# Two units' decay factors loaded once and spread by TensorE, with a new instruction sequence

## Chip, cores and metric

The kernel runs on one core of a Trainium2 chip. The metric is the device time of one execution in microseconds (us), the median of several runs. Engines are called as in the profile: PE is TensorE (PEld its weight loads), DVE is VectorE, ACT is ScalarE, POOL is GpSimd, SP is SyncE, which here only issues DMAs. "SP's queue", "ACT's queue" and "POOL's queue" are the DMA queues that these engines issue to.

## What is computed

A chunked state-space layer (batch 4, 8 heads, 768 steps, head dimension 32, state 16) is followed by a SiLU feed-forward block (256 to 2048 to 256) on its 3072 output rows:

```python
cum = np.cumsum(log(clip(a, 1e-6, 1)), axis=-1)          # within a chunk
L = np.exp(cum[..., :, None] - cum[..., None, :]) * causal
y = (einsum(C, B) * L) @ x + (C @ state) * exp(cum)
state = exp(sum(la)) * state + sum(B x x * exp(cum[-1] - cum))
...
h = y_rows @ w_in
out = (h * (1 / (1 + exp(-h)))) @ w_out
```

`a`, `B`, `C` and `x` are float32. The two weight matrices are float64, and the kernel reads them as pairs of 32-bit words.

## The kernel before

**Units.** The work is cut into 12 units of 256 steps, three for each batch element; a unit has four chunks of 64 steps. The feed-forward part takes units two at a time: a pair has 512 rows. The first pair (units 0 and 1) is multiplied in plain float32, the other five in a split form with three passes (h, l, d).

**The order is written out.** The string `SCHEDULE` is a list of steps such as `E,0,0` or `Ln,1,1,1,0`. A loop calls the function of each step, and each engine runs its instructions in the order in which they were issued. Steps of different engines have no order but by their data and their buffers. `SLOTS` says which buffer of a pool each new tile takes; a buffer taken again makes its new writer wait for the last reader.

**The steps of a unit u**, with the names used below:
- `Ln,u,i,k` loads half k of B (i = 0) or C (i = 1) with time on the partitions; `Lt,0,1,g` loads a quarter of unit 0's C in another layout; `Lx,u,k` loads half of x. A step's last number is its queue: 0 SP, 1 ACT, 2 POOL.
- `E,u,k` (DVE, a scan of 512 elements) builds the decay matrix of half k from a. `P` or `P01` (DVE, a scan of 260) builds the running products of a within each chunk.
- `T,u,i` transposes on DVE, `tp,u` on PE (units 0 to 2). `tq,u` and `ce,u,e` (ACT) copy the results out, `ce` masked for even or odd heads. `C,u` multiplies C by the running products, `B,u,k` B by the last column of the decay matrix (POOL).
- `g0,u` and `D,u` or `gd,u` (PE) form C times B and B times x; `M,u,w` (DVE) multiplies by the decay; `S,u,t` (DVE) carries the state from chunk to chunk; `SM,u,e` (ACT) masks it; `Y,u` (PE) forms the unit's output. `X0` or `y` copies that out (ACT).

**The weights.** `lw,n` (n = 0 to 15) loads a block of 512 KB. `u,n` and `v,n` (ACT), `w,n,0` to `w,n,2` (DVE) and `W,n` (POOL) turn it into float32. `H,n` (ACT), `Wl,n` (POOL), `Wd,n` (ACT) and `We,n` (a DMA on POOL's queue) make the split parts.

**The feed-forward part.** `s,u,j` is the first product of unit u (0 or 1) with weight block j, in 8 PE instructions; `si,u,j` its SiLU. `n,k` is k products of 2 PE instructions each of the second matrix for the first pair. `a,G,i`, `d,G,i` and `f,k` are the same for the other pairs. PE thus has a fixed list of work, and what can vary is how early it starts and how often it waits.

**a, for units 0 and 1.** The decay factors of the later units come through DRAM copies that the kernel writes itself (`ir`, `AA`, `AD`, then `La` and `Lp`). For units 0 and 1 they are made in two ways. `ip,u` (line 346) loads a unit's a to all 128 partitions, 16 copies of each head, 128 KB for each unit; `P01,u,0` (line 442) clamps it and `P01,u,1` (line 446) scans it. `ia` (line 342) loads the same values once more, 16 KB, as 32 rows; `A` (line 415) clamps them, `AT` transposes them on PE, `AU` copies them out, `as,u,k` (line 466, one on DVE, three on ACT) repeats each value 64 times, and `ab,u,k` (line 471) turns that in four PE transposes into a PSUM tile that holds on each row the factors of its chunk. `E` scans that tile.

`z,k,m` (lines 408 and 410) are products on constant data that feed nothing: k of 512 columns, m of 64.

Of the kernel before, what the change touches and what calls it, by code (L numbers as in the profile page):

```python
# [13 lines left out]
ALU = mybir.AluOpType  # L14
# [4 lines left out]
c1 ip,0,0 Ln,0,0,0,1 ci ia lw,0 z,1 cp cI z,1 ch z,1 z,0,6 Lt,0,1,2,1 z,0,6 z,0,6 z,1 Lt,0,1,0,1 Lt,0,1,3,1 z,1  # L19
Lt,0,1,1,1 cd lw,2 co z,1 Ln,0,0,1,1 z,1 Ln,1,0,0,0 P01,0,0 ct A ip,1,0 z,1 P01,0,1 Lx,0,0,0 Lx,0,1,0 AT u,0 AU  # L20
Ln,1,0,1,0 ca z,1 as,0,0 z,1 as,1,1 z,1 ab,0,0 Ln,1,1,0,0 z,0,6 cP as,0,1 w,0,0 T,0,1 Ln,1,1,1,0 C,0 as,1,0 Lx,1,0,0
z,0,6 ab,1,1 w,0,1 v,0 E,0,0 ab,0,1 ce,0,0 z,0,6 tp,0 ce,0,1 tq,0 g0,0 v,2 u,2 B,0,0 E,0,1 Lt,3,1,3,0 E,1,1 B,0,1 D,0
M,0,1 ab,1,0 Lx,1,1,0 w,2,0 S,0,0 M,0,0 S,0,1 w,2,1 B,1,1 lw,1 S,0,2 SM,0,1 SM,0,0 w,2,2 P01,1,0 tp,1 tq,1 lw,3 lw,10
lw,4 ce,1,1 ir,3 ce,1,0 W,2,2,0 Y,0 X0,0,0 E,1,0 X0,0,1 S,0,3 g0,1 u,1 P01,1,1 W,2,2,1 B,1,0 D,1 w,0,2 S,1,0 ir,2
S,1,1 W,0,2,0 S,1,2 lw,9 M,1,1 W,0,2,1 s,0,2 s,0,0 w,1,0 H,2 ir,1 ir,0 v,1 Wd,2 Lt,3,1,0,0 Wl,2 si,0,2 M,1,0 C,1
SM,1,0 SM,1,1 Y,1 v,3 w,1,1 u,3 u,10 si,0,0 w,1,2 W,1,2,0 X0,1,0 W,1,2,1 w,3,0 S,1,3 u,4 w,10,0 w,4,0 X0,1,1 s,0,1
lw,8 w,3,1 AA,0 v,4 Ln,2,0,0,0 u,9 Ln,2,0,1,0 w,3,2 v,9 w,4,1 w,4,2 s,1,0 s,1,2 AA,1 W,4,1,0 si,1,0 Lt,3,1,1,0 v,10
w,10,1 s,1,1 si,0,1 s,0,4 u,8 si,1,2 Ln,2,1,0,0 AD,4 H,4 Ln,2,1,1,0 w,9,0 s,1,4 W,3,1,0 w,9,1 lw,5 Wd,4 v,8 H,3
Lt,3,1,2,0 w,8,0 si,1,1 lw,11 tp,2 w,8,1 s,1,3 si,0,4 H,0 AD,0 si,1,4 w,8,2 v,5 u,5 lw,6 si,1,3 w,9,2 s,0,3 w,10,2
La,2,0,0 W,8,1,0 u,11 Lp,2,0 T,3,1 w,11,0 n,1 w,11,1 n,1 La,2,1,0 v,6 Lx,2,0,0 n,1 v,11 Lx,2,1,0 w,5,0 Wl,0 w,5,2  # L30
ce,2,1 tq,2 W,9,1,0 n,2 w,11,2 si,0,3 u,6 Lt,3,0,3,0 ce,2,0 E,2,1 Wl,4 lw,7 W,10,1,0 n,1 E,2,0 lw,12 AD,1 n,1 v,7 n,1
w,5,1 P,2 C,2 g0,2 B,2 W,5,1,0 gd,2 b,2,0 La,3,0,0 M,2,1 b,2,1 Lt,3,0,1,0 Lx,3,0,0 La,3,1,0 AD,2 u,7 u,12 Ln,3,0,1,0
W,11,1,0 S,2,0 w,6,0 Lt,3,0,2,0 w,7,2 Lt,3,0,0,0 Lt,4,1,0,0 M,2,0 Ln,3,0,0,0 n,1 Lt,4,1,1,0 Lp,3,0 ce,3,0 S,2,1 S,2,2
H,11 lw,14 w,7,0 w,7,1 n,2 s,0,5 ce,3,1 w,6,2 SM,2,1 E,3,0 SM,2,0 Y,2 Lx,3,1,0 si,0,5 n,1 v,12 n,1 W,7,1,0 n,1 H,1 H,9
E,3,1 lw,13 y,2,0 n,1 y,2,1 s,0,7 B,3 xh,2 x,2,0 T,3,0 H,5 g0,3 Wd,0 w,6,1 P,3 H,10 Lt,4,0,3,0 w,12,2 gd,3 La,4,0,0
si,0,7 b,3,0 M,3,1 w,12,0 Wd,9 Lt,4,0,1,0 Lt,4,0,2,0 b,3,1 La,4,1,0 S,3,0 S,3,1 W,6,1,0 Lt,4,1,2,0 s,0,6 Wl,11 si,0,6
v,13 C,3 M,3,0 S,3,2 w,12,1 Wl,5 Lt,4,1,3,0 SM,3,0 SM,3,1 x,2,1 u,13 H,8 Lp,4,0 n,1 We,0 s,1,6 W,12,1,0 Y,3 T,4,1
lw,15 w,13,2 n,2 Wl,3 y,3,0 Ln,4,0,0,0 Lt,4,0,0,0 y,3,1 xh,3 n,1 w,13,0 Lx,5,1,0 x,3,0 x,3,1 S,3,3 a,1,0 E,4,1
Ln,4,0,1,0 si,1,6 s,1,5 w,13,1 We,2 v,15 Lx,4,0,0 P,4 AD,3 n,1 u,15 ce,4,1 W,13,1,0 T,4,0 w,15,0 ax,1,0 u,14 E,4,0
d,1,0 ce,4,0 si,1,5 H,6 v,14 w,14,0 H,7 dg,1,0 Lx,4,1,0 Wl,10 H,12 w,14,1 C,4 w,15,1 Lp,5,0 s,1,7 w,14,2 B,4 si,1,7  # L40
g0,4 W,14,1,0 h,1,0 gd,4 M,4,1 n,1 Lx,5,0,0 b,4,0 b,4,1 S,4,0 n,1 Wd,1 S,4,1 S,4,2 Wd,12 Lt,5,0,2,0 Wl,1 We,1 n,2
M,4,0 Lt,5,1,3,0 Wd,5 SM,4,0 La,5,1,0 n,1 SM,4,1 Y,4 Wl,8 w,15,2 e,1,0 n,1 Wd,3 Wl,7 y,4,1 H,13 f,1 a,1,1 y,4,0 We,4
W,15,1,0 Ln,5,0,0,0 S,4,3 Wl,9 Wd,6 a,1,2 We,9 ax,1,1 We,3 Wd,8 n,1 Wd,11 We,8 La,5,0,0 l,1,0 n,1 E,5,1 H,14 La,6,0,0
Lt,5,1,2,0 E,5,0 Wd,7 ax,1,2 Lt,5,1,0,0 n,1 Wd,14 d,1,2 Lt,5,1,1,0 d,1,1 Ln,5,0,1,0 dg,1,2 n,1 T,5,1 dg,1,1 h,1,2
h,1,1 ce,5,0 We,11 a,1,4 ax,1,4 f,1 n,1 Lt,6,1,0,0 H,15 B,5 Lt,5,0,1,0 We,5 e,1,1 Ln,6,0,1,0 n,1 a,1,3 Vn,0 d,1,4
l,1,1 f,1 Lt,6,1,1,0 Wd,13 Vn,1 f,2 ax,1,3 Wl,6 xh,4 P,5 d,1,3 Wl,13 C,5 ce,5,1 f,3 Lt,5,0,0,0 dg,1,4 f,2 Wl,14 dg,1,3
Lt,5,0,3,0 La,6,1,0 f,1 o,0,0,2 gd,5 T,5,0 g0,5 Wl,12 f,2 Lt,6,1,3,0 E,6,0 f,3 Lt,6,1,2,0 f,2 Wl,15 f,1 o,0,1,2 M,5,1
Lx,6,1,0 Wd,10 f,1 a,1,5 x,4,0 f,2 T,6,1 b,5,0 h,1,3 e,1,2 f,1 S,5,0 Lt,6,0,3,0 We,10 l,1,2 f,2 O,0,1,2,3,0 b,5,1
S,5,1 O,0,0,2,3,0 f,1 h,1,4 Ln,6,0,0,0 ax,1,5 M,5,0 d,1,5 l,1,3 O,0,1,2,0,0 ce,6,1 dg,1,5 S,5,2 f,1 We,12 Lp,6,0 E,6,1
We,7 SM,5,0 O,0,0,2,0,0 Lt,6,0,1,0 x,4,1 SM,5,1 f,2 Lt,6,0,0,0 f,1 P,6 Lt,6,0,2,0 f,1 Wd,15 f,3 e,1,3 We,13 Y,5 f,2  # L50
y,5,1 f,1 y,5,0 e,1,4 xh,5 a,1,7 ax,1,7 f,2 B,6 f,1 Lt,7,1,2,0 f,1 h,1,5 f,2 We,6 d,1,7 f,2 T,6,0 x,5,0 f,1 Lt,7,1,3,0
x,5,1 f,1 Lx,6,0,0 l,1,4 f,2 ce,6,0 dg,1,7 La,7,0,0 g0,6 gd,6 b,6,0 M,6,1 e,1,5 f,1 M,6,0 f,1 b,6,1 S,6,0 a,2,1 a,1,6
S,6,1 f,1 S,6,2 ax,2,1 f,1 Lx,7,1,0 ax,1,6 O,0,1,2,2,0 SM,6,0 Ln,7,0,0,0 d,2,1 f,1 d,1,6 f,3 La,7,1,0 Lt,7,0,3,0
Ln,7,0,1,0 f,3 Lt,7,0,2,0 dg,2,1 C,6 dg,1,6 l,1,5 h,1,7 f,1 SM,6,1 h,1,6 O,0,0,2,2,0 f,2 Y,6 y,6,0 f,2 Lt,7,1,1,0
Lt,7,1,0,0 f,2 We,14 y,6,1 l,1,6 f,1 a,2,0 f,1 ax,2,0 f,3 T,7,1 e,1,6 f,2 h,2,1 f,2 d,2,0 a,2,3 f,1 We,15 O,0,1,2,1,0
Lt,7,0,1,0 f,1 E,7,0 f,1 E,7,1 f,2 l,1,7 dg,2,0 e,1,7 Lt,7,0,0,0 a,2,2 h,2,0 e,2,0 Lx,8,1,0 f,2 Lp,7,0 ax,2,3 f,2
ce,7,1 l,2,0 ax,2,2 ce,7,0 S,6,3 f,2 P,7 d,2,3 dg,2,3 f,2 O,0,0,2,1,0 La,8,1,0 f,2 T,7,0 f,1 l,2,1 f,3 d,2,2 Va,1,0
xh,6 f,2 Va,1,1 f,1 Lt,8,1,1,0 Lt,8,1,2,0 Lx,7,0,0 Lt,8,1,3,0 Vd,1,0 f,1 dg,2,2 Lt,8,0,2,0 f,1 C,7 La,8,0,0 f,1 B,7
x,6,1 Vd,1,1 gd,7 g0,7 f,2 M,7,0 f,1 Lt,8,0,0,0 e,2,1 b,7,0 Lt,8,0,3,0 M,7,1 b,7,1 Lt,8,1,0,0 f,3 S,7,0 Ln,8,0,1,0
h,2,2 T,8,1 l,2,2 a,2,4 ax,2,4 Lt,9,1,2,0 f,1 Lt,8,0,1,0 S,7,1 a,2,5 S,7,2 f,2 d,2,4 f,1 Lt,9,1,0,0 ax,2,5 f,1 SM,7,0  # L60
d,2,5 f,1 Lp,8,0 f,2 SM,7,1 Lt,9,1,3,0 x,6,0 T,8,0 f,2 dg,2,4 E,8,1 f,2 ce,8,1 dg,2,5 e,2,2 E,8,0 Y,7 f,3 y,7,1 f,2
a,2,7 Ln,8,0,0,0 y,7,0 f,3 h,2,3 h,2,4 f,2 a,2,6 ce,8,0 e,2,3 ax,2,7 S,7,3 f,2 Lx,8,0,0 l,2,3 La,9,1,0 f,1 xh,7
Lt,9,0,1,0 Lt,9,0,2,0 d,2,7 ax,2,6 d,2,6 P,8 h,2,5 e,2,4 La,9,0,0 f,7 Lt,9,1,1,0 x,7,0 dg,2,7 Lx,9,1,0 B,8 dg,2,6
E,9,0 gd,8 g0,8 l,2,4 f,2 o,1,0,2 b,8,0 f,2 S,8,0 f,2 M,8,1 f,2 l,2,5 h,2,6 a,3,1 M,8,0 C,8 Ln,9,0,0,0 b,8,1 f,1 S,8,1
T,9,1 f,1 ax,3,1 Lt,10,1,0,0 f,1 a,3,0 f,1 e,2,5 ax,3,0 f,1 e,2,6 S,8,2 x,7,1 f,4 d,3,1 f,2 ce,9,0 f,2 SM,8,1 l,2,6
d,3,0 O,1,0,2,3,0 E,9,1 f,2 h,2,7 f,2 Lt,10,1,1,0 dg,3,1 Lt,10,1,2,0 dg,3,0 Lx,9,0,0 f,1 SM,8,0 f,1 Y,8 f,1 Lp,9,0
# [819 lines left out]
```

## Time and profile before

| | |
|---|---|
| median of 3 runs | 332.06 us (331.10 to 332.59) |
| the profiled execution | 331.95 us, of which the trace's span is 330.2 us |
| mean granted TensorE clock | 0.998 |
| PE busy | 319.5 us (97%) |
| DVE busy | 240.8 us (73%) |
| ACT busy | 207.4 us (63%) |
| POOL busy | 88.8 us (27%) |
| DMA | 30.83 MB in 95,817 packets |
| a for the running products, `ip` | 2 loads of 128 KB |
| a for the decay matrices, `ia` | 1 load of 16 KB |
| `ab`'s transposes, line 471 | 16 of 128x128 |

The table is to be read with the time line beside it. A busy share is a mean over the whole span; the profile's second part gives it in 40 slices of 8.25 us, and windows of any size can be asked for. The chain of waits goes back from the last instruction and names at each step what released it.

### The profile page before, as it was taken

What the parts mean: (1) busy time and instruction counts of PE and PEld (TensorE: products, weight loads), DVE (VectorE), ACT (ScalarE), POOL (GpSimd) and SP (SyncE); (2) the same over time, 40 slices, a digit from 0 to 9 for tenths busy, and PEclk for the clock granted to TensorE, in tenths of its full rate; (3) what the DMA queues carried; (4) which work ended last, traced back from release to release, by engine and by line L of the source; (5) the groups of instructions that cost most, each with busy time, mean ns of one, the idle gap of its engine ahead of it and who ended that gap; (6) DMA issues with size and microseconds to landing.
All of it is one profiled execution on the core that took longest, in us unless ns stands there. A gap on an engine that the chain in (4) does not pass through costs nothing.

```text
span 330.2 us, 7573 instructions
## 1 busy us (share of the span) xinstructions
PE 319.5 (97%) x3086; PEld 243.8 (74%) x3086; DVE 240.8 (73%) x314; ACT 207.4 (63%) x323; POOL 88.8 (27%) x96
## 2 busy tenths in 40 slices
PE   7699999999999999999999999999999999999995
PEld 3478746665667778877878878778887788888883
DVE  4979899999957972978589469688648534555563
ACT  3689928578787558565756566655664737474441
POOL 2367853978969510020010100200000000000000
PEclk9999999999999999999999999999999999999999
DMA  6799699594696991412422441450003100005002
GB/s 170 121 339 222 184 219 206 142 193 102 129 185 98 196 173 35 99 47 45 99 25 64 74 97 24 92 102 11 2 0 65 18 0 2 0 0 89 0 0 64
DMA packets 95817, 30.83 MB, mean 93 GB/s; under 512 B 80088, under 2 KB 87000, under 8 KB 95784
## 3 DMA queue, kind: packets, MB, share of 16 engines
q1 hardware_dynamic: 90632, 25.58, 36.1%
q0 software_dynamic: 2480, 4.39, 7.4%
q10 hardware_dynamic: 2672, 0.39, 0.7%
q8 instruction: 24, 0.39, 0.5%
q14 instruction: 9, 0.07, 0.1%
HBM read 22.81 MB, written 3.34 MB: 79 GB/s over the span
## 4 chain that ended last, share of the span: by engine, by line
PE 88%; DVE 4%; DMA 3%; SPq 2%; ACT 1%; issue 1%; POOL 1%; DVEq 0%
PE hp L766 28%; PE ga L785 17%; PE gb L785 17%; PE hp L676 7%; PE o_ps L766 6%; PE hp L744 5%; PE ga L616 2%; PE ga L556 2%; PE ga L607 1%; DMA raw<-in_moe_w_in_dram 1%; DVE s2k L292 1%; DMA s2k<-in_C_dram 1%; PE ga L542 1%; PE gb L607 1%; SPq L258 1%
## 5 line engine op out<-in xcount | busy, mean ns | idle before, releaser
L766 PE MATMUL hp<-r4k,s2k 128*128 128x512 f32 x400 | 113.3, 394 | 0.0
L766 PEld LDWEIGHTS hp<-r4k,s2k 128*128 128x128 f32 x400 | 74.4, 188 | 16.5 <-issue 0.6
L633 DVE SCALAR_TENSOR_TENSOR r4k<-r4k,r4k 128x1024 fp32r<-128x1024 f32 x40 | 50.9, 1278 | 30.1 <-PE hp L766 16.8
L636 DVE SCALAR_TENSOR_TENSOR r4k<-r4k,r4k 128x1024 fp32r<-128x1024 f32 x40 | 49.7, 1247 | 27.2 <-ACT r4k L812 15.2
L785 PE MATMUL ga<-raw,s2k 128*128 128x512 f32 x240 | 62.8, 397 | 0.0
L785 PE MATMUL gb<-raw,s2k 128*128 128x512 f32 x240 | 61.8, 393 | 0.0
L785 PEld LDWEIGHTS ga<-raw,s2k 128*128 128x128 f32 x240 | 44.6, 188 | 12.2 <-issue 1.2
L785 PEld LDWEIGHTS gb<-raw,s2k 128*128 128x128 f32 x240 | 44.4, 188 | 11.2 <-ACT gb L796 1.0
L812 ACT ACTIVATE r4k<-r4k 128x1024 fp32r<-128x1024 f32 x40 | 41.8, 1055 | 4.3 <-PE hp L766 2.6
L796 ACT ACTIVATE ga<-ga 128x1024 f32<-128x1024 f32 x20 | 20.2, 1009 | 32.6 <-PE ga L785 32.6
L796 ACT ACTIVATE gb<-gb 128x1024 f32<-128x1024 f32 x20 | 20.2, 1008 | 17.9 <-PE gb L785 16.9
L766 PE MATMUL o_ps<-r4k,s2k 128*128 128x512 f32 x80 | 31.2, 396 | 0.0
L744 PE MATMUL hp<-r4k,s2k 128*128 128x512 f32 x64 | 29.8, 600 | 0.7 <-POOL s2k L310 0.7
L676 PE MATMUL hp<-r4k,s2k 128*128 128x256 f32 x128 | 29.5, 382 | 0.0
L489 POOL TENSOR_TENSOR BT<-bn,ab 128x256 f32<-128x256 f32 x10 | 9.4, 939 | 72.0 <-PE hp L766 27.8
L676 PEld LDWEIGHTS hp<-r4k,s2k 128*128 128x128 f32 x128 | 23.9, 190 | 5.0 <-issue 1.0
L310 POOL TENSOR_TENSOR s2k<-s2k,s2k 128x512 uint32<-128x512 uint32 (+1 forms) x19 | 24.1, 1277 | 11.3 <-DVE s2k L299 5.8
L520 POOL TENSOR_TENSOR cw<-ct,pfx 128x256 f32<-128x256 f32 x9 | 9.5, 1053 | 64.8 <-DVE pfx L453 64.8
L806 ACT ACTIVATE r4k<-ga 128x1024 f32<-128x1024 f32 x20 | 20.5, 1024 | 9.8 <-PE ga L785 4.3
L481 DVE TENSOR_TENSOR_SCAN ab<-ab,diag 128x512 f32<-128x512 f32 x20 | 26.0, 1316 | 0.8 <-DMA ab<-az 0.8
L806 ACT ACTIVATE r4k<-gb 128x1024 f32<-128x1024 f32 x20 | 20.4, 1022 | 6.8 <-PE gb L785 5.7
L319 POOL TENSOR_TENSOR s2k<-s2k,s2k 128x512 fp32r<-128x512 f32 x16 | 24.0, 1568 | 0.8 <-ACT s2k L314 0.8
(118 smaller groups left out, 399.0 us busy)
## 6 DMA issues: line engine op xcount, KB each, us to landing
ab<-az SPq DMA_DIRECT2D x20, 256.0 KB
raw<-in_moe_w_in_dram SPq DMA_DIRECT2D x8, 512.0 KB
raw<-in_moe_w_out_dram SPq DMA_DIRECT2D x8, 512.0 KB
s2k<-s2k POOLq DMA_DIRECT2D x16, 256.0 KB, 5.4
out_dram<-r4k SPq DMA_DIRECT2D x44, 64.0 KB
xt<-in_x_dram SPq DMA_DIRECT2D x20, 128.0 KB
pz<-ac SPq DMA_DIRECT2D x10, 130.0 KB
bn<-in_B_dram SPq DMA_DIRECT2D x20, 64.0 KB
```

Source lines behind the costliest of these rows:

```text
L310: nc.gpsimd.tensor_tensor(out=dst[:, :, fs].bitcast(U32), in0=u[:, :, fs], in1=v[:, :, fs], op=ALU.add)
L319: nc.gpsimd.tensor_tensor(out=t, in0=f32(WK[n, "h"]), in1=WT[n], op=ALU.add)
L481: nc.vector.tensor_tensor_scan(out=o, data0=src, data1=diag.rearrange("p h t -> p (h t)"), initial=0.0, op0=ALU.mult, op1=ALU.add)
L633: nc.vector.scalar_tensor_tensor(out=l, in0=f32(h), scalar=BACK, in1=y, op0=ALU.mult, op1=ALU.add)
L636: nc.vector.scalar_tensor_tensor(out=d, in0=f32(h), scalar=-(BACK + 1.0), in1=y, op0=ALU.mult, op1=ALU.subtract)
L676: nc.tensor.matmul(out=hp[:, i], lhsT=WT[j][:, kc, 128 * i:128 * i + 128], rhs=XM[:, 2 * kc:2 * kc + 2, u], start=(kc == 0), stop=(kc == K ...
L744: nc.tensor.matmul(out=NP["o"][m], lhsT=WT[8 + f // 2][:, f % 2, 128 * m:128 * m + 128], rhs=GT[0, f // 2][:, f % 2], start=(f == 0), stop ...
L766: nc.tensor.matmul(out=ACC[P, 2 * (p == "d") + m], lhsT=WK[8 + f // 2, p][:, f % 2, 128 * m:128 * m + 128], rhs=rhs, start=(f == 0 and p ! ...
L785: nc.tensor.matmul(out=o, lhsT=WK[j, q][:, kc, 128 * i:128 * i + 128], rhs=xs[:, 2 * kc:2 * kc + 2], start=(start and q == "h" and kc == 0 ...
L796: nc.scalar.activation(t, t, AF.Copy, scale=1.0 + Z)
L806: nc.scalar.activation(g, t, AF.Silu, scale=BACK)
L812: nc.scalar.activation(t, GT[G, i], AF.Copy, scale=-LESS * Z)
```

## The change

The decay factors of units 0 and 1 are loaded once, to 8 partitions instead of 128, and PE spreads them with matrices of zeros and ones (`pick` and `spread`):

```diff
-    ach = small([32, 2, Q])
-    aT = small([128, 8, 4])
+    ar, pr = small([8, H, Q]), small([H, 2 * UT])
+    pick, spread = small([8, 4 * 128]), small([H, 128])
-    pa = [small([128, UT]) for _ in range(2)]
-    pz01, pfx01 = ([small([128, 4, Q + 1]) for _ in range(2)] for _ in range(2))
+    pz01 = [small([H, 4, Q + 1]) for _ in range(2)]
+    pfx01 = [small([128, 4, Q + 1]) for _ in range(2)]
     def i_a():
-        nc.sync.dma_start(out=ach, in_=...ap=[[Q, 8], [2 * S, 4], [S, 2], [1, Q]])
+        nc.sync.dma_start(out=ar, in_=...ap=[[Q, 8], [S, H], [1, Q]])
-    def i_p(u, q):
-        QUEUES[q].dma_start(out=pa[u], in_=...ap=[[S, H], [0, N], [1, UT]])
+    def i_p(q):
+        QUEUES[q].dma_start(out=pr, in_=...ap=[[S, H], [1, 2 * UT]])
+    def band(t, n, w):
+        nc.gpsimd.memset(t, 1.0)
+        nc.gpsimd.affine_select(out=t, in_=t, pattern=[[1, n]], compare_op=ALU.is_ge,
+                                fill=0.0, base=0, channel_multiplier=-w)
+        nc.gpsimd.affine_select(out=t, in_=t, pattern=[[-1, n]], compare_op=ALU.is_ge,
+                                fill=0.0, base=w - 1, channel_multiplier=w)
     def f_A():
-        nc.vector.tensor_scalar(out=ach, in0=ach, scalar1=1.0, scalar2=1e-6, ...)
-        nc.vector.memset(ach[:, :, 0:1], 0.0)
+        nc.vector.tensor_scalar(out=ar, in0=ar, scalar1=1.0, scalar2=1e-6, ...)
+        nc.vector.memset(ar[:, :, 0:1], 0.0)
-    def f_AT(): ...
-    def f_AU(): ...
-    def f_AS(u, k): ...
+    def f_PA(u):
+        nc.gpsimd.tensor_scalar(out=pz01[u][:, :, 1:], in0=pr[:, UT * u:UT * u + UT]..., ...)
+    def f_pb(u):
+        AB["p", u] = t = take("hp", [128, 4, Q + 1])
+        nc.tensor.matmul(out=t..., lhsT=spread, rhs=pz01[u]..., start=True, stop=True)
+    def f_P01(u):
         nc.vector.tensor_tensor_scan(out=PFX[u]...,
-                                     data0=pz01[u]...,
+                                     data0=AB["p", u]...,
     def f_Ab(u, k):
         AB[u, k] = t = take("hp", [128, H, Q])
-        for j in range(4):
-            nc.tensor.transpose(out=t[:, 2 * j:2 * j + 2]..., in_=AS[u, k][:, j]..., identity=ident)
+        f = 128 * (2 * u + k)
+        nc.tensor.matmul(out=t..., lhsT=pick[:, f:f + 128], rhs=ar..., start=True, stop=True)
```

The new steps are `cs` and `c2`, which build `pick` (8 x 512) and `spread` (8 x 128) on POOL with `band`; `PA,u`, the clamp of 8 x 256 values on POOL; and `pb,u`, the product that spreads them to 128 partitions in PSUM. The steps `ip,u`, `P01,u,0`, `P01,u,1`, `AT`, `AU` and the four `as` go; `ip` and `P01,u` are there once for the load and once for each unit's scan.

The other steps are the same in number (480 products `f`, 32 products `n`, 11 long and 36 short products of `z`), but `SCHEDULE` and `SLOTS` are replaced as a whole. The new sequence begins:

```
cs ca Ln,0,0,1,1 cI ci c1 z,1 Ln,0,0,0,1 Lt,0,1,0,1 ip,0 c2 PA,0 z,1 ch z,1 cp z,0,6 ia Lt,0,1,1,1 lw,0 A z,0,6
Lt,0,1,3,1 z,0,6 z,1 z,1 z,1 z,1 z,1 cd pb,0 cP ab,0,0 Lt,0,1,2,1 P01,0 E,0,0 T,0,1 PA,1 v,0 ab,0,1 z,1 z,1 E,0,1 lw,2
Ln,1,1,0,0 Lx,0,0,0 z,1 z,0,6 u,0 ce,0,0 z,0,6 Lx,0,1,0 B,0,0 C,0 B,0,1 z,0,6 Ln,1,0,0,0 Ln,1,0,1,0 ce,0,1 tp,0 co
Ln,1,1,1,0 Lx,1,1,0 ab,1,1 u,2 tq,0 ct Lx,1,0,0 w,0,0 w,2,0 w,0,1 E,1,1 g0,0 lw,1 D,0 B,1,1 M,0,1 S,0,0 M,0,0 S,0,1
w,2,1 v,2 lw,3 ab,1,0 tp,1 ce,1,0 S,0,2 w,2,2 E,1,0 SM,0,0 ir,2 SM,0,1 lw,10 S,0,3 W,2,2,0 Y,0 ce,1,1 tq,1 X0,0,0
B,1,0 W,2,2,1 X0,0,1 v,1 u,1 pb,1 P01,1 w,0,2 lw,4 g0,1 W,0,2,0 u,3 D,1 S,1,0 S,1,1 S,1,2 ir,0 H,2 M,1,1 w,1,0 ir,1
W,0,2,1 w,1,2 ir,3 M,1,0 SM,1,0 w,1,1 v,3 C,1 s,0,2 s,0,0 Ln,2,1,1,0 SM,1,1 S,1,3 W,1,2,0 u,10 w,3,2 Y,1 W,1,2,1
```

The old one begins:

```
c1 ip,0,0 Ln,0,0,0,1 ci ia lw,0 z,1 cp cI z,1 ch z,1 z,0,6 Lt,0,1,2,1 z,0,6 z,0,6 z,1 Lt,0,1,0,1 Lt,0,1,3,1 z,1
Lt,0,1,1,1 cd lw,2 co z,1 Ln,0,0,1,1 z,1 Ln,1,0,0,0 P01,0,0 ct A ip,1,0 z,1 P01,0,1 Lx,0,0,0 Lx,0,1,0 AT u,0 AU
Ln,1,0,1,0 ca z,1 as,0,0 z,1 as,1,1 z,1 ab,0,0 Ln,1,1,0,0 z,0,6 cP as,0,1 w,0,0 T,0,1 Ln,1,1,1,0 C,0 as,1,0 Lx,1,0,0
z,0,6 ab,1,1 w,0,1 v,0 E,0,0 ab,0,1 ce,0,0 z,0,6 tp,0 ce,0,1 tq,0 g0,0 v,2 u,2 B,0,0 E,0,1 Lt,3,1,3,0 E,1,1 B,0,1 D,0
M,0,1 ab,1,0 Lx,1,1,0 w,2,0 S,0,0 M,0,0 S,0,1 w,2,1 B,1,1 lw,1 S,0,2 SM,0,1 SM,0,0 w,2,2 P01,1,0 tp,1 tq,1 lw,3 lw,10
lw,4 ce,1,1 ir,3 ce,1,0 W,2,2,0 Y,0 X0,0,0 E,1,0 X0,0,1 S,0,3 g0,1 u,1 P01,1,1 W,2,2,1 B,1,0 D,1 w,0,2 S,1,0 ir,2
S,1,1 W,0,2,0 S,1,2 lw,9 M,1,1 W,0,2,1 s,0,2 s,0,0 w,1,0 H,2 ir,1 ir,0 v,1 Wd,2 Lt,3,1,0,0 Wl,2 si,0,2 M,1,0 C,1
```

PE's list from unit 2 to the second pair, before (first line) and after (second line), without the other engines' steps:

```
tp,2 s,1,3 s,0,3 n,1 n,1 n,1 n,2 n,1 n,1 n,1 g0,2 gd,2 n,1 n,2 s,0,5 Y,2 n,1 n,1 n,1 n,1 s,0,7 g0,3 gd,3 s,0,6 n,1 s,1,6 Y,3 n,2 n,1 a,1,0 s,1,5 n,1 d,1,0
s,1,3 tp,2 n,1 n,1 n,1 n,1 s,0,3 n,2 n,2 g0,2 gd,2 n,1 s,0,5 n,3 n,1 n,1 Y,2 s,0,7 n,1 g0,3 gd,3 s,0,6 n,1 s,1,6 Y,3 n,1 s,1,5 a,1,0 n,1 n,1 d,1,0
```

At the end of the list the order on each engine is the same but for two neighbouring DVE steps (`Vt,5,1,2` and `Vt,5,1,3`), the order of the last stores, and single products `f` about the last pair's steps.

## The prediction

> **What bounds the kernel now.** First the busy shares by slice (each 8.25 us):
>
> ```profile
> PE   7699999999999999999999999999999999999995
> DVE  4979899999957972978589469688648534555563
> ```
>
> PE is full from the third slice to the last, DVE from the second to the ninth. Windows of the trace sharpen this (start:end, length, then busy time and instruction count of PE, PEld, DVE, ACT, POOL, then clock, DMA share, GB/s):
>
> ```profile
> 8.30:16.50 8.20, 5.38 (x152) 3.85 (x152) 8.20 (x16) 5.06 (x13) 3.07 (x6) 1.00 0.78 120
> 24.80:41.00 16.20, 16.20 (x73) 13.11 (x72) 14.56 (x19) 15.51 (x31) 13.15 (x12) 1.00 0.79 204
> 46.00:50.00 4.00, 3.77 (x36) 2.16 (x35) 3.87 (x6) 1.97 (x6) 3.62 (x4) 1.00 1.14 197
> 50.00:54.00 4.00, 3.59 (x104) 2.43 (x103) 3.93 (x8) 3.29 (x9) 1.47 (x1) 1.00 0.84 114
> 64.00:67.00 3.00, 2.28 (x91) 1.62 (x91) 3.00 (x6) 2.86 (x8) 2.60 (x3) 1.00 0.87 178
> 82.00:120.00 38.00, 38.00 (x367) 27.88 (x371) 30.86 (x33) 28.20 (x44) 27.11 (x26) 1.00 0.87 158
> 120.00:320.00 200.00, 200.00 (x1732) 160.61 (x1719) 133.32 (x157) 120.77 (x160) 9.76 (x10) 1.00 0.22 44
> 320.00:330.20 10.20, 6.46 (x29) 4.81 (x27) 3.42 (x8) 1.58 (x3) 0.00 (x0) 0.93 0.24 51
> ```
>
> PE is never idle from 82 to 320 us, nor from 24.8 to 41. Between 41 and 74 it idles 1.38 us: 0.23, 0.41 and 0.72 in the three windows shown, 0.02 elsewhere. The last 10.2 us hold 3.74, in the tail. So the time is the moment at which PE's dense work begins, a fixed list of work, about 1.4 us of waits, and the tail. The chain of waits gives that moment (start, length, what):
>
> ```profile
> 11.08 4.26 DMA s2k<-in_C_dram
> ...
> 15.39 0.51 PE o_ps L500 x2
> ...
> 17.23 0.39 ACT r4k L646
> 17.62 0.04 issue
> ...
> 19.01 3.65 PE hp L676 x16
> ```
>
> PE's second pair of transposes for unit 1 (`tp,1`, line 500) waits for unit 1's C, which lands at 15.34; then come `Y,0`, the copy-out on ACT, `g0,1`, `D,1`, and at 19.01 the first product `s,0,2`. The time line shows what DVE and ACT wait for meanwhile:
>
> ```profile
> 1.93 0.35 POOL L362 TENSOR_SCALAR_AFFINE_SELECT ident<-ident 128x128 f32<-128x128 f32 x1 [0.29 <-DVE ident L361]
> ...
> 3.57 0.44 ACTq L243 DMA_DIRECT2D s2k<-in_B_dram  x1
> 4.04 1.28 ACT L358 ACT_TABLE_LOAD   x1 [4.04 <-DMA s2k<-in_B_dram]
> ...
> 7.24 0.67 ACT L283 ACTIVATE s2k<-raw 128x512 f32<-128x512 f32 x1 [1.71 <-DMA raw<-in_moe_w_in_dram]
> ...
> 7.95 0.43 DVE L292 TENSOR_SCALAR s2k<-s2k 128x512 f32<-128x512 f32 x1 [1.38 <-ACT s2k L283]
> ...
> 9.11 3.43 DVE L481 TENSOR_TENSOR_SCAN ab<-hp,diag 128x512 f32<-128x512 f32 x3
> ...
> 14.94 0.64 ACT L594 ACTIVATE sm<-st,par 128x96 f32<-128x96 f32 x2 [2.72 <-DVE st L586]
> ...
> ```
>
> DVE stands until 7.95 behind `w,0,0`, whose data ACT can only make once block 0 lands at 7.22; so `E,0,0` starts at 9.11. ACT's masked copy `SM,0` starts at 14.94, on DVE's S.
>
> **The parts of the change, against the profiled execution's 331.95 us** (span 330.2 and 1.75 around it; the median of the runs is 332.06, 0.11 more).
>
> *Loads.* Gone are 256 KB on SP's queue, one half ahead of blocks 0 and 2, the other ahead of unit 0's x; 16 KB come for them. From 6 to 8 us the DMA moved 252 GB/s, so each 128 KB is 0.5 us of it. Also, unit 0's second half of B (ACT's queue, issued at 3.57) was still awaited by a PE weight load at 10.30: its small packets shared the DMA with the blocks. Now it is issued first, some 2.8 us earlier; I count half of its 64 KB, by its neighbours' 0.95 us (PE awaited unit 0's x until 12.55, and three such loads land from there to 15.34), as 0.45. Unit 1's C, still the last of B and C, then lands at 15.34 - 0.5 - 0.5 - 0.45 = 13.9. Bounds: 15.34 (the relief comes to nothing) and 13.0 (also the 0.45 us by which two shorter issues bring the blocks forward, and the other half).
>
> *POOL.* `cs` is a memset (8 columns took 0.10, 260 took 0.32, so 0.54 for 512) and two selects (0.19 for 8 columns, 0.35 for 128, so 0.86): 2.3. With `ca` 0.10, `cI` 0.35, `c1` 0.54, `c2` 0.2 + 2 x 0.35 and `PA,0` at 0.5 (half of line 429's 1.07 for 512), from 0.9, `PA,0` ends at 5.6. POOL idled from 3.3 to 9.0, which hides it; but unlike before, PE's `pb,0` now waits for it.
>
> *PE.* Each `ab` becomes one float32 product of 512 columns, two instructions at 0.454 (line 744, 8 in 3.63) = 0.91 for 0.60 to 0.66; two `pb` add 0.46 each. This is +2.0 us before 19, where PE idles 5.1 us of 16.5 and runs fillers; without that cover it would be +2.0 on the end. `pb,0` and `ab,0,0` end at 7.0.
>
> *DVE and ACT.* DVE loses two clamps (0.30 each), `AU` (0.17) and `as` (0.43) and pays 0.22 more in `A`: -0.98. ACT loses 3 x 0.55; `ct` with its table load (1.28 and 0.20) moves from ACT's idle start to behind `tq,0`, near 10.7 to 12.2, where `v,2` comes next, wanted by DVE at 14.1: nothing, and 1.5 if that cover were gone. That PSUM now feeds `P01` I price at nothing, since line 481's scan takes 1.14 from PSUM and 1.17 from SBUF; bounds 0 and 0.1 each. `E,0,0` starts at 7.0 instead of 9.11. But `w,0,0`, `w,2,0` and `w,0,1` now lie between `E,0,1` and `E,1,1`: 7.0 + 3 x 1.14 + `T` 0.55 + 3 x 0.34 = 12.0 for `M,0,1` (before 12.47), and `S,0,2` ends near 14.1 (before 14.9).
>
> *The start, summed.* ACT's `ce,1,0` is now queued ahead of `SM,0`, and needs `tp,1`. From C at 13.9: `tp,1` 0.51, `ce` 0.42, `SM` 0.64, four hand-overs of 0.05: `Y,0` at 15.65 (before 15.83). Behind it nothing is new on the path: `ce,1,1` and `tq,1` lie under `Y,0`, and `pb,1` under the 0.47 us that PE waits for ACT's copy. The distance from `Y,0` to `s,0,2` stays 3.18: 18.83. **Start: -0.2**, with ends -0.9 (C at 13.0 and DVE's S then deciding) and +1.3 (C at 15.34: `tp,1`, `ce` and `SM` in series put `Y,0` at 17.1).
>
> *The middle.* PE's list is the same but for order. The 0.23 at 46.2 was `gd,2` waiting for `B,2` behind `E,2`; now `w,11,1`, `w,11,2` and `T,3,1` (0.34 + 0.6 + 0.5) come behind `E,2` and 1.4 us of DVE work less ahead of it. The 0.41 was `Y,2` behind the states and `SM,2`; between `gd,2` and `Y,2` PE now has `s,0,5` (1.82) and 6 products (0.91) instead of 3: 2.7 us more to do. The 0.72 at 66 was a product waiting for POOL's `W,12`; the steps of DVE ahead of it are 1.2 us shorter. All three would go: -1.36. But other margins get thin. Adding up PE's list and DVE's list with the trace's durations, `SM,3` and `Y,3` (64.4) meet within 0.3 us, `x,3,0` and its product `a,1,0` (68.5) within 0.4; the first product of block 8 comes 1.8 us earlier in PE's list while `Wl,4` (1.45) now stands ahead of `W,8` on POOL; `AD,3` (0.6), a DMA issue on POOL's queue, moves ahead of `W,9`; `lw,7` moves behind `Lp,2` and two `Lt` on SP's queue, so that ACT's `u,7` and `v,7` move too. In its favour, the `ir` loads go ahead of `lw,9` on SP's queue, and POOL's `AA,0` waited 2.07 us for them. I take half: **middle: -0.65**, ends -1.36 and +1.4 (one step of POOL's length newly waited for).
>
> *The rest.* From 82 us on PE has no wait to lose, and the tail's order is the same: 0. Sum: 331.95 - 0.2 - 0.65 = **331.1**.
>
> **Rivals.**
> *A: the relief of the DMA is larger.* C at 13.0, DVE's S deciding (`Y,0` at 14.9, -0.9), and all three waits gone (-1.36): 329.7. For it: 1 us of transfers goes from a stretch in which the DMA is 0.92 to 0.96 busy (4 to 10 us). Against: from 10 us on it is 0.63 or less in places, and packets may set the pace.
>
> *B: slower.* The quarter of unit 0's C that is issued last on ACT's queue (`Lt,0,1,2`) comes late, and `T,0,1` holds DVE between the two scans. Before, the four quarters were behind one load of B; now they are behind both. If it lands where that queue's last load was awaited before, at 10.3, `T,0,1` starts at 10.3 and not 8.1, DVE's dense run shifts by 2.2, `S,0,2` ends at 16.3, `SM,0` at 17.0, `s,0,2` starts at 20.25 (+1.25); DVE stays behind, and `E,2` with it, so that the middle's 1.36 is kept and some 0.8 more comes (2.2 less the 1.4 won there): 331.95 + 1.25 + 0.8 = 334.0. It decides from a landing after 8.1 on. For it: 64 KB took from 4.0 to 10.3 in that queue. Against: now both loads of B are issued before any block is under way.
>
> *C: PE starts at half rate.* The first three fillers took 1.46 us, 0.49 each, later ones 0.27. If PE stood idle long enough before `Y,0` to fall back, the first 3.5 us of products (the slow stretch lasted from 1.34 to about 4.9) would lose half: +1.75, 332.9 on the forecast. Against: PE idled 1.69 us before 15.39 and ran `s,0,2` at the full 0.228 a pass. [...]
>
> *D: the loads were hidden anyway*, C lands as before, and the middle trades wait for wait: 332.0.
>
> **Chances.** Forecast 0.40, A 0.30, B 0.22, C 0.04, D 0.04. Within 0.5% (330.4 to 333.7), about what runs of this kernel can tell from no change, lie the forecast (but for 0.02 on either side), C and D: 0.44. Faster: A and 0.02, 0.32. Slower: B and 0.02, 0.24. The forecast alone spans 330.0 to 332.5. The range reaches to A and B, from 329.4 to 334.1; beyond it lie both ends at once of the unknown costs.
>
> **What would show it.** Right: `E,0,0` at about 7, unit 1's C at 13 to 14.3, `s,0,2` at 18.4 to 19.2, PE idle under 1 us between 41 and 74, none from 82 to 320. Wrong: a wait of DVE for `Lt` before `T,0,1` (B); `SM,0` ready long before `ce,1,0` with C after 15; passes of 256 columns above 0.3 us at `s,0,2` (C); a new wait above 1 us before `Y,3`, `a,1,0` or the first `n`; PE idle anywhere past 82.

## The result: slower by 1.3%, and PE at half its clock for 17 us

The changed kernel takes 336.18 us (4 runs, 336.08 to 337.64), the kernel before beside it 332.32 (4 runs, 331.10 to 333.36): a ratio of 1.0128 [1.0083, 1.0173]. The profiled execution took 337.64, its span is 335.6, and its mean granted clock is 0.973, as in all four runs (before: 0.998). The forecast was 331.1, the range ended at 334.1. One run of the kernel before, 337.50 us beside kernels 5 to 8, counts as a slow one and is left out of every figure below.

The page's 40 slices of 8.4 us, after:

```profile
PE   8999999999999999999999999999999999999995
DVE  3866899989938995577948768958646674153863
PEclk9658999999999999999999999999999999999999
```

The third row before was:

```profile
PEclk9999999999999999999999999999999999999999
```

PE's row looks better than before: it is full from the second slice to the last but one, and PE's busy time has grown from 319.5 us to 329.2. The changed kernel's third row says why that is no good news: the granted clock is 0.6, 0.5 and 0.8 in slices 2 to 4, where the kernel before had nothing but nines. Windows of the changed kernel, with the columns as in the prediction (the third number from the end is the clock):

```profile
8.30:16.50 8.20, 8.20 (x93) 3.33 (x91) 7.29 (x14) 3.78 (x7) 2.54 (x6) 0.61 1.06 209
9.50:10.00 0.50, 0.50 (x16) 0.48 (x16) 0.50 (x2) 0.20 (x1) 0.39 (x2) 1.00 1.08 105
10.00:10.50 0.50, 0.50 (x11) 0.44 (x7) 0.50 (x1) 0.50 (x2) 0.50 (x1) 0.65 0.75 75
10.50:11.00 0.50, 0.50 (x3) 0.18 (x2) 0.50 (x2) 0.50 (x2) 0.17 (x2) 0.50 1.16 109
...
26.50:27.00 0.50, 0.50 (x3) 0.41 (x2) 0.50 (x2) 0.00 (x0) 0.50 (x2) 0.50 0.34 60
27.00:27.50 0.50, 0.50 (x4) 0.45 (x3) 0.50 (x2) 0.00 (x0) 0.50 (x1) 0.79 0.50 168
27.50:28.00 0.50, 0.50 (x4) 0.45 (x3) 0.50 (x1) 0.00 (x0) 0.49 (x1) 1.00 1.05 397
...
64.00:67.00 3.00, 2.41 (x52) 1.90 (x41) 2.86 (x6) 1.48 (x4) 3.00 (x3) 1.00 0.96 165
...
82.00:120.00 38.00, 37.75 (x434) 26.74 (x435) 29.82 (x36) 27.98 (x48) 28.66 (x27) 1.00 0.79 146
```

Every window reads 1.00 or 0.50 except those in which the clock changes, and their mean gives the moment: 0.65 over 10.0 to 10.5 is 0.15 us at full and 0.35 at half, so it fell at 10.15; 0.79 over 27.0 to 27.5 puts the return at 27.21. Between them lie 17.06 us. And in 8.3 to 16.5, where PE had been busy 5.38 us of 8.20, it is now busy for all of it, at a mean clock of 0.61. The chain of waits:

```profile
6.21 0.91 PE hp L442 x2
7.12 1.72 PE hp L464 x4
8.83 0.75 PE o_ps L413 x3
9.59 0.69 PE o_ps L415 x18
10.27 0.62 PE o_ps L493 x2
10.89 2.00 PE hp L464 x2
...
14.59 2.00 PE hp L464 x2
16.58 1.04 PE o_ps L493 x4
...
22.56 5.97 PE hp L669 x16
```

Before, this part of the chain was a landing of C, an ACT copy, and PE only at its end. Now it is PE alone: from 4.9 us on it waits for nobody, and the others wait for it. `s,0,2` begins at 22.56, not 19.01: 3.55 us. Its 16 passes (a pass is one PE instruction of a product) take 5.97 and not 3.65, since the first ten still run at half the clock: 2.3 more. That is 5.9 us lost by 28.5; the span grew by 5.4, so some 0.5 is won later. The time line says who waits:

```profile
3.89 2.31 PE L413 MATMUL o_ps<-s2k 128*128 128x512 bf16 x5
6.14 0.98 PE L442 MATMUL hp<-s2k,s2k 8*128 8x260 f32 x2
6.96 1.88 PE L464 MATMUL hp<-s2k,s2k 8*128 8x512 f32 x4
8.77 0.82 PE L413 MATMUL o_ps<-s2k 128*128 128x512 bf16 x3
...
10.82 2.07 PE L464 MATMUL hp<-s2k,s2k 8*128 8x512 f32 x2
```

The first fillers (line 413) ran at half rate, 0.46 each, those at 8.77 took 0.27: the rate came up in between. The changes of the granted clock found ahead of the tail of an execution lie whole multiples of 3.41 us apart, to within 0.03 (17.06 here; 20.49 in kernel 2 below; 3.41, 6.83 and 10.24 in kernel 4; 3.41 in kernel 7). So I cut the time into stretches of 3.41 us; one stretch before 10.15 is 6.74, which fits the rise, as the passes of `ab` start 0.43 apart from 6.96 on. That the work within a stretch sets the clock at its end is my estimate from these times; no record shows it. `ab,0,0` and `ab,0,1` (line 464) took 1.88 for four passes, `ab,1,1` 2.07 for two. DVE's `E,1,1` started at 12.93 behind that (10.85 by the forecast's own sum), and ACT stood 4.12 us for `tp,1`, which PE reached at 16.51.

### The profile page after: what moved, and what is told of

It is laid out like the page before. It is cut to its first block, busy times and chain, and to the rows that moved or that the text cites. A ratio compares the mean times of both kernels' runs of the same rounds, so it can differ in the third digit from the quotient of the medians.

```text
span 335.6 us, 7571 instructions
## 1 busy us (share of the span) xinstructions
PE 329.2 (98%) x3081; PEld 248.3 (74%) x3081; DVE 236.5 (70%) x310; ACT 206.9 (62%) x321; POOL 91.3 (27%) x104
## 3 DMA queue, kind: packets, MB, share of 16 engines
HBM read 22.56 MB, written 3.34 MB: 77 GB/s over the span
## 4 chain that ended last, share of the span: by engine, by line
PE 94%; DVE 3%; issue 1%; ACT 1%; DVEq 0%
PE hp L759 28%; PE gb L778 16%; PE ga L778 16%; PE hp L669 8%; PE hp L737 7%; PE o_ps L759 5%; PE ga L549 2%; PE ga L609 2%; PE ga L600 2%; PE hp L464 2%; PE o_ps L413 1%; PE gb L600 1%; PE ga L535 1%; DVE ab L474 1%; PE o_ps L493 1%
## 5 line engine op out<-in xcount | busy, mean ns | idle before, releaser
L759 PEld LDWEIGHTS hp<-r4k,s2k 128*128 128x128 f32 x400 | 74.3, 188 | 16.1 <-issue 0.7
L626 DVE SCALAR_TENSOR_TENSOR r4k<-r4k,r4k 128x1024 fp32r<-128x1024 f32 x40 | 49.9, 1253 | 15.6 <-ACT r4k L805 10.1
L669 PE MATMUL hp<-r4k,s2k 128*128 128x256 f32 x128 | 32.1, 404 | 0.6 <-issue 0.6
L669 PEld LDWEIGHTS hp<-r4k,s2k 128*128 128x128 f32 x128 | 25.6, 203 | 7.2 <-issue 2.6
L474 DVE TENSOR_TENSOR_SCAN ab<-ab,diag 128x512 f32<-128x512 f32 x20 | 24.3, 1229 | 4.7 <-DMA ab<-az 4.7
L513 POOL TENSOR_TENSOR cw<-ct,pfx 128x256 f32<-128x256 f32 x9 | 10.5, 1167 | 54.4 <-DVE pfx L454 27.6
```

The costliest lines, as they stand in the source:

```text
L474: nc.vector.tensor_tensor_scan(out=o, data0=src, data1=diag.rearrange("p h t -> p (h t)"), initial=0.0, op0=ALU.mult, op1=ALU.add)
L626: nc.vector.scalar_tensor_tensor(out=l, in0=f32(h), scalar=BACK, in1=y, op0=ALU.mult, op1=ALU.add)
L669: nc.tensor.matmul(out=hp[:, i], lhsT=WT[j][:, kc, 128 * i:128 * i + 128], rhs=XM[:, 2 * kc:2 * kc + 2, u], start=(kc == 0), stop=(kc == K ...
L759: nc.tensor.matmul(out=ACC[P, 2 * (p == "d") + m], lhsT=WK[8 + f // 2, p][:, f % 2, 128 * m:128 * m + 128], rhs=rhs, start=(f == 0 and p ! ...
```

## The experiments

Theory R: products on 8 of the 128 rows do not keep the clock up, so that it falls behind a stretch filled with `pb` and `ab` although PE is busy. Rivals: the clock answers to PE's load as such (a fall under more work), to the new order, or to something else that fell into this time. In the time line, whose starts lie 0.07 us before the chain's, `s,0,2` begins at 18.94 before and at 22.49 after; that number is given for each kernel.

**1. The same products on 128 rows.** Same sequence, same number of PE instructions, columns and passes; only 120 rows of zeros are added, and cleared once:

```diff
-    ar, pr = small([8, H, Q]), small([H, 2 * UT])
-    pick, spread = small([8, 4 * 128]), small([H, 128])
-    pz01 = [small([H, 4, Q + 1]) for _ in range(2)]
+    ar, pr = small([128, H, Q]), small([H, 2 * UT])
+    pick, spread = small([128, 4 * 128]), small([128, 128])
+    pz01 = [small([128, 4, Q + 1]) for _ in range(2)]
```

`ar` is cleared on POOL in `cs`, `pz01` on DVE in `cp`. That second clearing comes behind the clamp of unit 0, so unit 0's running products are zeros in this kernel and in the next one.

> Theory (few rows): PE's clock is granted by how much of the array its products use, and products of 8 rows count for next to nothing, so that the stretch from 6.8 to 10.2 us looks idle although PE is busy. Here the same products get 128 rows, 120 of them zeros, with the same number of instructions and columns. Expected: granted clock 1.00 from 7 us on (mean above 0.99), passes of ab at 0.43 us throughout, s,0,2 at 18.3 to 19.4 instead of 22.6, 330.3 to 332.5 us. Rival (order and waits: the new sequence leaves PE without work at the wrong moments): the clock falls at 10.2 us as before, mean 0.973, 335.5 to 337.5 us.

Measured: 331.61 us (10 runs), ratio to the kernel before 0.9986 [0.9971, 1.0000], clock 0.998 in the profiled run and 0.997 to 1.000 in all ten, `s,0,2` at 18.68. The time line of this kernel:

```profile
6.94 2.13 PE L464 MATMUL hp<-s2k,s2k 128*128 128x512 f32 x4
...
10.60 1.02 PE L464 MATMUL hp<-s2k,s2k 128*128 128x512 f32 x2
...
13.65 1.12 PE L464 MATMUL hp<-s2k,s2k 128*128 128x512 f32 x2 [0.70 <-DVE ab L474]
14.61 0.60 PE L493 MATMUL o_ps<-ident,s2k 128*128 128x128 f32 x4
```

`ab,1,1` takes 1.02 for its two passes instead of 2.07, and PE again waits for DVE and not the other way round. The whole loss is gone with the rows: neither the order nor the number of products nor PE's load makes it.

**2. 32 rows.** The same kernel with 32 in the place of 128, to see whether they are enough.

> As the run with 128 rows, with 32 rows, a quarter of the array. If only full rows count, or rows in proportion with a bar above a quarter: the clock falls to 0.5 near 10 us, mean 0.97 to 0.98, 334.5 to 337 us. If any group of 32 rows counts as busy: clock 1.00, 330.3 to 332.5 us. Rival (order and waits): as with 8 rows, 335.5 to 337.5 us.

Measured: 338.35 us (one run), clock 0.969; the clock fell at 8.05 and came back at 28.54, 20.49 us or six times 3.41 later, and the time lies above all that was expected. In this run 32 rows did not hold the clock. PE also stood idle for 0.66 us in the 3.41 us before the fall, waiting for DVE, so the rows may not be all of it here.

**3. The kernel before with its fillers on 8 rows.** If R holds, the old kernel loses by it too: its fillers are there in the same number, and feed nothing.

```diff
-            nc.tensor.matmul(out=t, lhsT=idle[:, 0:128], rhs=idle, start=True, stop=True)
+            nc.tensor.matmul(out=t, lhsT=idle[0:8, 0:128], rhs=idle[0:8], start=True, stop=True)
```

(and the short ones likewise).

> The kernel before, with every filler product on 8 rows instead of 128, same columns, same count, same places. Theory (few rows): the fillers no longer bring the clock up; PE runs at 0.5 until some 3 to 7 us after the dense products begin at about 19 to 21 us; 336 to 340 us. Rival (order and waits: PE is as busy as ever): clock 1.00 and 331 to 333.5 us.

Measured: 333.89 us (one run), 2.1 above the 331.78 of the kernel before on that chip; `s,0,2` at 21.40. Its time line:

```profile
3.83 2.31 PE L408 MATMUL o_ps<-s2k 8*128 8x512 bf16 x5
...
7.08 1.44 PE L408 MATMUL o_ps<-s2k 8*128 8x512 bf16 x3 [0.33 <-DVE s2k L424]
...
10.27 1.97 PE L471 MATMUL hp<-ident,s2k 128*128 128x128 f32 x8
```

The same groups of the kernel before:

```profile
6.03 0.81 PE L408 MATMUL o_ps<-s2k 128*128 128x512 bf16 x3 [0.40 <-DVE s2k L424]
...
8.49 1.18 PE L471 MATMUL hp<-ident,s2k 128*128 128x128 f32 x8 [0.72 <-ACT s2k L466]
```

Fillers at 7.08 still take 0.48 each, where they took 0.27, and eight transposes take 1.97 instead of 1.18. The direction is R's, the size smaller than expected (the time alone, one run, would not show it: the kernel before reached 333.25 on that chip): a short pass of line 616 goes from 0.32 to 0.22 at 18.6, so PE was at full rate before `s,0,2`. In this run fillers on 8 rows did not bring the clock up; the kernel's own work then did.

**4. After, with eight fillers of 128 rows behind `ab,0,1`.** If the falling stretch needs only more work of full height, they should help.

```diff
-... v,0 ab,0,1 z,1 z,1 E,0,1 ...
+... v,0 ab,0,1 z,1 z,1 z,8 E,0,1 ...
```

> The changed kernel with 8 more fillers of 512 columns and 128 rows (1.7 us) behind ab,0,1, near 9.3 us, where the clock was lost at 10.2. Theory (few rows, a window must hold enough work on full rows): the fall at 10.2 is gone; whether the next windows (13.6, 17.0), which hold ab,1,1, g0,0 and ab,1,0, keep it is open: 332 to 335 us if they do, 335 to 338 if it falls one or two windows later. Rival (order and waits): no change in the fall at 10.2 us, 336 to 338 us.

Measured: 338.57 us (one run), longer than any case expected, clock 0.979. Windows:

```profile
8.00:8.50 0.50, 0.50 (x4) 0.26 (x4) 0.50 (x2) 0.00 (x0) 0.00 (x0) 0.91 0.93 141
...
9.00:12.00 3.00, 3.00 (x8) 0.91 (x6) 2.20 (x4) 1.46 (x3) 1.71 (x4) 0.53 1.06 122
...
18.50:19.00 0.50, 0.50 (x23) 0.50 (x23) 0.50 (x1) 0.50 (x2) 0.49 (x1) 0.65 1.09 401
...
28.50:29.00 0.50, 0.50 (x3) 0.38 (x3) 0.50 (x1) 0.00 (x0) 0.50 (x2) 0.61 0.78 180
```

By the same reading the clock falls at 8.41, returns at 11.82, falls at 18.65 and returns at 28.89: steps of 3.41, 6.83 and 10.24, that is one, two and three times 3.41. The first fall came too early for the added fillers: the stretch that it closes (5.00 to 8.41) held `pb,0` and four passes of `ab`, some 2.4 us on 8 rows. The next one, from 8.41, held nothing but the fillers, and the clock came back at its end. So in this run the clock came back behind 3.41 us of fillers on 128 rows, but these missed the first stretch and cost time. Where the stretches lie differs between the profiled executions (the first fall came at 8.05 in kernel 2, 8.41 here and 10.15 in the changed kernel, which are no multiples of 3.41 apart), so that fillers at one place, as here, can come too late.

**5 to 7. Rows again, one product at a time.** `pz01` is now cleared ahead of the clamp (in `c1`), so that all is computed. Kernel 5 has 128 rows throughout, kernel 6 has 64, and kernel 7 has `ab` on 128 rows but `pb` on 8.

> The run with 128 rows, with the clearing of the padded tiles put ahead of the clamp, so that unit 0's running products are whole. It is the change without its loss of clock. Theory (few rows): clock 0.998, s,0,2 at 18.5 to 18.9, 331.0 to 332.0 us, a ratio to the kernel before of 0.996 to 1.000. If the zeros of the first run had helped the clock: a fall to 0.5 at some point, 334 us or more.

> The same with 64 rows, half of the array. If what counts is the share of rows and the bar lies between a quarter and a half: clock 0.998, 331 to 332 us. If only nearly full rows count: the clock falls between 8 and 11 us as with 32 rows, mean 0.97, 336 to 339 us.

> Only the four ab products get 128 rows; the two pb products stay at 8. pb is 0.5 to 0.7 us of a stretch of 3.4. Theory (few rows, by the share of such a stretch): clock 0.998, 331 to 332 us. If a single product of few rows is enough: the clock falls as in the changed kernel, 335 to 338 us.

Measured, all on one chip (the kernel before there: 332.92, 14 runs):

| kernel | us | clock | `s,0,2` at |
|---|---|---|---|
| 5: 128 rows | 330.97 (8 runs, 330.71 to 331.49), ratio 0.9949 [0.9929, 0.9969] | 0.997 | 17.88 |
| 6: 64 rows | 330.75 (one run) | 1.000 | 18.11 |
| 7: `ab` 128, `pb` 8 | 334.06 (one run) | 0.993 | 20.48 |

Kernels 5 and 6 came out slightly faster than expected. In one run 64 rows held the clock (1.000) as 128 did in eight (0.997 to 1.000). Kernel 7 lies between the two times that were expected for it; in its windows

```profile
20.50:21.00 0.50, 0.50 (x9) 0.43 (x3) 0.29 (x2) 0.50 (x2) 0.50 (x1) 0.74 1.25 251
21.00:21.50 0.50, 0.50 (x3) 0.41 (x2) 0.47 (x2) 0.03 (x1) 0.50 (x2) 0.50 1.19 342
...
24.00:24.50 0.50, 0.50 (x4) 0.43 (x3) 0.50 (x3) 0.00 (x0) 0.36 (x1) 0.85 1.17 302
```

the clock falls at 20.74 for one stretch, to 24.15; the stretch before it held `pb,1` at 18.04 and 0.58 us in which PE was idle. At the start, too, `ab,0,0` and `ab,0,1` took 3.56 us for their four passes, where kernel 5 needed 1.88: the rate came up later. That needn't be due to `pb,0`: in the changed kernel, whose `pb,0` has 8 rows too, the same four passes took 1.88. So one run suggests that `pb` alone can cost a fall, but does not show it; the place of the stretches may be part of it, and the kernel before, which has no `pb`, shows lowered clocks in some of its runs too (0.985 to 0.988 in six, last section).

The chain of kernel 5 answers to the one shown before:

```profile
11.66 1.14 DVE ab L476
12.80 0.04 issue
12.85 1.12 PE hp L466 x2
13.97 0.45 PE o_ps L495 x4
...
14.51 0.47 ACT ce L510
14.98 0.54 ACT sm L589 x2
15.52 0.04 issue
...
17.95 3.65 PE hp L671 x16
```

Unit 1's C is no longer in it; the last landing in this chain is that of unit 0's C, at 8.29. `tp,1` (13.97) stands on PE behind `ab,1,0`, which waits for DVE's `E,1,1`; then `ce,1,0`, `SM,0`, and the rest of PE's list up to `s,0,2`.

**8. Kernel 5 in a better order.** Three moves: `S,0,2` ahead of `w,2,1` on DVE, `tp,1` ahead of `ab,1,0` on PE, and `Wl,4` behind `W,8` on POOL (PE had waited 0.51 us for that `W,8` at 36.5 in kernel 1), with two buffers exchanged to fit:

```diff
-w,2,1 v,2 lw,3 ab,1,0 tp,1 ce,1,0 S,0,2 w,2,2 E,1,0 SM,0,0 ...
+S,0,2 v,2 lw,3 tp,1 ab,1,0 ce,1,0 w,2,1 w,2,2 E,1,0 SM,0,0 ...
-... w,9,1 Wl,4 si,0,4 w,8,1 s,1,3 W,8,1,0 w,9,2 ...
+... w,9,1 si,0,4 w,8,1 s,1,3 W,8,1,0 Wl,4 w,9,2 ...
```

> The run with 128 rows and two steps moved: S,0,2 ahead of w,2,1 and tp,1 ahead of ab,1,0, since SM,0 starts right behind S,0,2 there (15.68 behind 15.62), worth up to 0.35 us on s,0,2; and Wl,4 behind W,8 on POOL, since PE idles 0.51 us near 36.5 for W,8. Expected: 0.4 to 0.9 us less than the run with 128 rows: 330.6 to 331.4 us. If DVE or the W,2 halves decide: 0.0 to 0.4 less.

Measured: 330.42 us (8 runs, 329.95 to 330.96), ratio 0.9927 [0.9903, 0.9951], clock 1.000, `s,0,2` at 17.56. Beside kernel 5 on the same chip that is 0.55 us less, though the two sets of runs overlap. In the traces 0.32 of it is there at `s,0,2`; the third move had nothing to win against kernel 5, where PE does not wait for `W,8`. Kernel 8 is 0.7% faster than the kernel before.

Its order also shows when unit 1's C lands, since PE gets to `tp,1` sooner:

```profile
12.70 0.33 PE L493 MATMUL o_ps<-ident,s2k 128*128 128x128 f32 x1 [0.23 <-DMA s2k<-in_C_dram]
```

## Why the prediction failed, and what of it held

**The step that failed** is the price of PE's new products: "+2.0 us before 19, where PE idles 5.1 us of 16.5 and runs fillers". By busy time the cover was there, and kernel 5, which pays for the same 12 passes, shows that they are hidden: `s,0,2` came 1.06 us earlier than before. What the sum left out is PE's rate: these products took the place of fillers on 128 rows, and on 8 rows they did not keep the clock up (0.5 from 10.15 to 27.21). Price of the step: nothing seen with 64 or 128 rows (`s,0,2` at 18.11 and 17.88, before 18.94), 5.9 us by 28.5 with 8.

**Rival C** was the right kind of case, with a chance of 0.04 and a price too small. It asked only whether PE "stood idle long enough", and was argued down with PE's idle time. A fall of the clock with PE idle is in the traces, in the tail: before, PE's last product ends at 326.91 and the clock goes to 0.5 at 328.75, after at 332.26 and 334.41. How long PE has to idle for it is not shown; before, the clock still read 1.00 from 13.60 to 15.40, where PE was busy 0.12 us of 1.80. But the fall at 10.15 came with PE busy, 5.25 us of the 5.25 from 4.90 on, and 8.20 of 8.20 in the window shown. C's sign came true, since the first ten passes at `s,0,2` took 0.46 each. The price of 1.75 counted the first products alone; what stood ahead of them at half rate (3.55 us) was twice as much. Its slow stretch at the start of the kernel before also ended nearer 4.5 than 4.9 us: the fillers there start at 3.84, 4.24, 4.58 and 4.80, so that their distance, 0.40 at first, is down to 0.22 from 4.58 on.

The changes in four kernels (after, 2, 4 and 7) lie 17.06, 20.49, 10.24, 6.83 and 3.41 us apart, and between them the clock is 0.5 or 1. The cause of this spacing is not shown.

**The loads and the start.** With the clock kept, this held, but for other reasons than given. Unit 1's C no longer sets the path: in kernel 5 `tp,1` found it there at 13.8 (forecast: 13.9), and in kernel 8 it was awaited only until 12.70, so that the relief there was 2.6 us, not the 1.45 of the sum and more than its bound of 13.0 allowed. DVE was slower than forecast: `E,0,0` at 7.44 rather than 7.0, `M,0,1` at 12.71 rather than 12.0, `SM,0` done at 15.52 where the sum had 15.6. One error of working hid behind that: the 3.18 us from `Y,0` to `s,0,2` contain 0.8 us of products (line 607 before) that don't need `SM,0` and were already done; from the end of `SM,0` it is 2.4. So `s,0,2` came at 17.95 in the chain, not 18.83, in kernel 5, and at 18.75 in kernel 1, where `E,0,0` began 0.8 us later, behind a clearing on DVE that waited for POOL until 5.42.

**POOL's new work** was priced too high and was hidden: a select on 512 columns took 0.60, not 0.86, and `PA,0` ended at 5.01, not 5.6. ACT's table load moved to 11.56, 1.28 us, where nothing waited for it, as forecast.

**The middle.** Forecast: PE idle under 1 us between 41 and 74. After: 0.59, of it the wait at 64 to 67 shown above; kernel 5: 0.20 (before 1.38). But 0.35 came back between 74 and 82 and 0.14 behind, and 0.36 at 22.6, none of them there before: 1.05 us of waits in all from `s,0,2` to 320, a gain of 0.3 and not 0.65. "None from 82 to 320" was wrong by 0.38 us in after.

**Rivals B and D.** The last quarter of C did land late, at 8.29 in kernel 5 and 8.51 in kernel 1, past the 8.1 from which it was to decide; but `E,0,0` was late too, and `T,0,1` followed it at once (8.58 in kernel 5, 9.15 in after). It cost nothing there. In kernel 8, where `E,0,0` began at 7.12, the landing at 8.39 let `T,0,1` start only at 8.41, 1.29 us behind `E,0,0` instead of 1.14: B's wait is there, and is worth 0.15 us. With the clock kept, kernel 5's 330.97 lies at the forecast's 331.1, in part by luck: the start gained 1.06 us where the sum had 0.2, and the waits behind it 0.3 where it had 0.65. Kernel 1's 331.61, with DVE's late start, lies between the forecast and D's 332.0. A's 329.7 was not reached in that order.

## What to carry to other kernels

In this kernel products on 8 of the 128 rows cost their time and, beyond it, the clock: 336.18 us at 0.973, against 330.97 at 0.997 with 128 rows (kernel 5) and 330.75 at 1.000 with 64 (kernel 6, one run). So read the granted clock before any busy share, and when short contractions are put into a stretch that is not full of other work, try them on 64 rows or more, with zeros in the rest; here that cost two clearings and no PE time (the first four passes of `ab` took 1.88 us on 8, 64 and 128 rows alike, in after and kernels 6 and 5). Look at the rows of a filler, not only at its time: with the fillers on 8 rows `s,0,2` came at 21.40 instead of 18.94 (kernel 3, one run). A busy PE at half its clock looked like a better used one: 329.2 us busy after, 319.5 before.

## What the hardware showed beyond that

- Zeros were enough here: in kernel 4 the clock came from 0.5 back to 1 at 11.82, at the end of a stretch that held only fillers, whose operands are all zeros, and with rows padded with zeros it read 0.998, 0.997, 1.000 and 1.000 in the profiled runs of kernels 1, 5, 6 and 8.
- For this mix of work one run with 32 rows lost the clock (0.969) and one with 64 kept it (1.000); it isn't settled whether rows count in proportion. Two of the falling stretches held about 1.0 to 1.3 us of full-height work in 3.41 (after: the fillers from 8.83 to 10.15; kernel 4: those before 5.6 and after 8.0), while before, PE was busy only 5.38 us of 8.20 and kept the clock (1.00); either reading fits.
- The granted clock in the records does not show the half rate at the start, nor the first rise: it reads 1.00 up to 10.0 us in after while the passes at 3.89 took 0.46, and 1.000 for the whole of kernel 3. There the length of a pass was the surer sign.
- The kernel before seems to pay now and then as well. Of its runs beside these experiments, the eight at clock 1.000 took 331.33 to 331.75 us, the six at 0.985 to 0.988 took 333.12 to 333.96. All runs of kernels 5 and 8 lie at 0.997 or above, so some 1.3 us of their distance to its median on that chip (332.92) may be this, and 0.6 and 1.2 us are left against its runs at clock 1.000 there (331.48 to 331.73). Which of its stretches fell isn't known, as only the profiled execution has a trace.
